# Copying two projections in time order, and multiplying them from strided reads on GpSimd

## The chip, the cores and the metric

The kernel runs on one core of one Trainium2 chip. The metric is the device time of one execution in microseconds (us), the median of several runs. Engines are named as the profile names them: PE (TensorE matmul), PEld (TensorE weight load), DVE (VectorE), ACT (ScalarE), POOL (GpSimd), SP (SyncE, which here only issues DMAs).

## What is computed

Two layers, one behind the other, on `x` and `f_logit` of shape (4, 6272, 256):

```
sig = 1/(1+exp(-f_logit));  f = lb + (1-lb)*sig;  i = 1-f
h[t] = f[t]*h[t-1] + i[t]*x[t]                       # recurrence over t, per batch and column
x1, x2, x3 = split(h @ w_proj)                       # 256 -> 3 x 256
conv = irfft(rfft(x2, S) * rfft(filter, S), S)       # circular convolution over t, S = 6272
out  = (x1 * conv * x3) @ w_out
```

## The kernel before, in words

The sequence length 6272 is 49 * 128. The convolution is done as a Fourier transform in two factors, so time t = 49*m + r is needed both as a run over t (for the recurrence) and as an array over (r, m), with m from 0 to 127 innermost (for the transform's output). Each of the four batches b passes through these stages:

- `hgrn(b)`: 13 chunks of 512 time steps. A chunk is loaded (`FL`, `XT`, two buffers each), ACT takes the sigmoid in place (L283), POOL multiplies x by it (L285, 128x1024 f32), PE transposes both (L294), ACT makes f (`fTs`, L306), DVE scans (L311) and writes h into `HA`. Then a copy called a wrap (L262 when it is POOL's, L257 when it is DVE's) puts h a second time into the buffer between the two halves of `HA`.
- `phase_p(b)`: 98 pairs of matmuls (L590) project h to x2 with weights read from `HA` by a stride of 49; ACT or DVE evict to `X2`. It waits for all scans and wraps of the batch.
- `phase_f1(b)`: first factor of the transform (L605), evicted by ACT or DVE into `A`, in `HA`.
- `mini(b)`: a small product for frequency zero (L620, L626, L630), which ends in `zm`.
- `units(b)`: 16 units u. In each, four matmuls (L649, the second factor), two DVE products with the filter `Hu` (L659, into `PP`, two buffers), one POOL copy of `zm` into `PP` (L652), 16 small matmuls back (L669) and one eviction to `Th` (L252 on ACT or L257 on DVE). After unit u comes `gate(b, u)`.
- `gate(b, u)`: for each chunk c of `GATES[u]` (10 values of m, that is 490 time steps; the last chunk has 8 and 392) and for each of two column halves `jb`: PE projects h to x1 and to x3 (L340, two matmuls each of 490 columns), ACT copies both from PSUM to `x1s` and `x3s` (L350, two buffers each), POOL writes `z = x1s * x3s` (L355) in f16 in the (r, m) layout. There are 13 chunks, so 52 ACT copies and 26 POOL products per batch.
- `phase_o(b)`: 13 groups: matmuls (L695), the DVE product with `z` (L702, which needs all of the batch's z), the projection by `w_out` (L712), eviction by ACT (L254), store.

The instruction order is written by `Plan`, a list scheduler that runs when the program is built: each `op` is given a cost in microseconds per engine allowed, and tags that it reads (`r`) and writes (`w`); the plan gives the next instruction to the engine where it can start first, by those costs. Each engine then runs its own instructions strictly in that order. A cost in the source is therefore no time of the chip, but it decides the order, and also the engine where two are allowed. PSUM is eight banks, handed out by the plan. In `hgrn(b+1)` the transposes of chunk c wait for the tag `("U", AFTER[c])`, the end of unit 2, 5, 7, 10, 12 or 15 of batch b, so that batch b+1 begins inside `units(b)`. The tag `qX` keeps the projections of `gate` in order, the tag `qT` the transposes of `hgrn`. The projections of `gate(b, u)` read the tag `("F", u)`, so they wait for the L649 matmuls of unit u.

Of the kernel before, what the change touches and what calls it, by code (L numbers as in the profile page):

```python
# [13 lines left out]
AOP = mybir.AluOpType  # L14
AF = mybir.ActivationFunctionType
# [9 lines left out]
Q = 49  # L25
# [3 lines left out]
NCHK = 13  # L29

AFTER = (2, 5, 7, 10, 12, 15)

GATES = [[u] if u < NCHK else [] for u in range(16)]
XR = 10
NEP = 128
UE = 8
# [2 lines left out]
ZS = 64.0  # L39
# [16 lines left out]
class Plan:  # L56
# [20 lines left out]
    def op(self, cost, fn, r=(), w=(), kb=0.0, table=None, take=0, src=None):  # L77
        preds = set()
        for t in r:
            if t in self.writer:  # L80
                preds.add(self.writer[t])
        for t in w:
            if t in self.writer:
                preds.add(self.writer[t])
            preds.update(self.readers.get(t, ()))
        me = len(self.ops)
        if src is not None:
            preds.add(src)
            self.ops[src]["users"].append(me)
        self.ops.append(dict(cost=cost, fn=fn, preds=preds, kb=kb, table=table, end=None,  # L90
                             eng=None, succ=[], take=take, src=src, users=[], at=None))
        for p in preds:
            self.ops[p]["succ"].append(me)
        for t in r:
            self.readers.setdefault(t, set()).add(me)
        for t in w:
            self.writer[t] = me
            self.readers[t] = set()
        return me
# [89 lines left out]
def kernel(  # L189
# [15 lines left out]
    op = plan.op  # L205
# [12 lines left out]
    W13 = konst.tile([128, 2, 512], F16, name="W13")  # L218
# [13 lines left out]
    x1s = konst.tile([128, 2, CH], F32, name="x1s")  # L232
# [5 lines left out]
    PS = psp.tile([128, 8, 512], F32, name="PS")  # L238

    def E(a, z):  # L240

        return [("E", u) for u in range(a // 1024, (z - 1) // 1024 + 1)]
# [6 lines left out]
    def copy(e, dst, src, scale=None):  # L249
        if e == "ACT":  # L250
            if scale is None:
                nc.scalar.copy(dst, src)  # L252
            else:
                nc.scalar.activation(dst, src, AF.Copy, scale=scale)  # L254
        elif e == "DVE":
            if scale is None:
                nc.vector.tensor_copy(dst, src)  # L257
            else:
                nc.vector.tensor_scalar(dst, in0=src, scalar1=scale, scalar2=None,
                                        op0=AOP.mult)  # L260
        else:
            nc.gpsimd.tensor_copy(dst, src)  # L262

    def either(n, runs=1.0):

        return {"ACT": 0.06 + runs * n / 1200.0, "DVE": 0.08 + runs * n / 960.0}

    count = dict(x=0, f=0, s=0, o=0)

# [1 line left out]
    def hgrn(b):  # L271
        for c in range(NCHK):
            t0 = c * CH
            nb = min(CH, S - t0) // 128
            n = nb * 128
            k = count["x"] % NX
            count["x"] += 1
            xt, ft = XT[:, k, 0:nb], FL[:, k, 0:nb]
            for dst, src, t in ((ft, f_logit, ("ft", k)), (xt, x, ("xt", k))):
                op({"SP": 0.5}, lambda e, dst=dst, src=src, t0=t0, n=n: nc.sync.dma_start(  # L280
                    dst, src[b, t0:t0 + n, :].rearrange("(j p) d -> p j d", p=128)),
                   w=[t], kb=n)
            op({"ACT": 0.1 + 0.213 * nb}, lambda e, ft=ft: nc.scalar.activation(  # L283
                ft, ft, AF.Sigmoid, scale=-1.0), r=["sin"], w=[("ft", k)], table="sigmoid")
            op({"POOL": 0.1 + 0.535 * nb}, lambda e, xt=xt, ft=ft: nc.gpsimd.tensor_tensor(  # L285
                xt, xt, ft, op=AOP.mult), r=[("ft", k)], w=[("xt", k)])

            late = [("U", AFTER[min(c, len(AFTER) - 1)])] if b else []
            for kh in range(2):
                cols = slice(kh * 128, kh * 128 + 128)  # L290

                def turn(e, p, src, cols=cols, nb=nb):
                    for j in range(nb):
                        nc.tensor.transpose(PS[:, p, j * 128:(j + 1) * 128], src[:, j, cols],  # L294
                                            iden[:])
                sT = op({"PE": 0.108 * nb}, lambda e, p, f=turn, s=ft: f(e, p, s),
                        r=[("ft", k), "iden"] + late, w=["qT"], take=1)
                uT = op({"PE": 0.108 * nb}, lambda e, p, f=turn, s=xt: f(e, p, s),
                        r=[("xt", k), "iden"], w=["qT"], take=1)
                j = count["f"] % 2  # L300
                count["f"] += 1
                fT = fTs[:, j, 0:n]
                t1 = HB[kh] + t0
                h = HA[:, t1:t1 + n]
                op({"ACT": 0.13 + n / 1200.0}, lambda e, p, fT=fT, n=n, kh=kh:
                   nc.scalar.activation(fT, PS[:, p, 0:n], AF.Identity,  # L306
                                        scale=nomc[:, kh:kh + 1], bias=1.0),
                   r=["om"], w=[("fT", j)], src=sT)
                init = 0.0 if c == 0 else HA[:, t1 - 1:t1]
                op({"DVE": 0.07 + 2.25 * n / 1000.0}, lambda e, p, h=h, fT=fT, n=n, init=init:  # L310
                   nc.vector.tensor_tensor_scan(h, fT, PS[:, p, 0:n], init, op0=AOP.mult,  # L311
                                                op1=AOP.add),
                   r=[("fT", j)] + ([("hn", kh, c - 1)] if c else []), w=[("hn", kh, c)],
                   src=uT)

                a, o = (t0, t0) if kh == 0 else (max(t0, S - E1), EW - S + max(t0, S - E1))
                z = min(t0 + n, E0) if kh == 0 else t0 + n
                if z <= a:
                    continue
                op({"DVE": 0.08 + (z - a) / 3840.0, "POOL": 0.1 + (z - a) / 1000.0},  # L320
                   lambda e, a=a, o=o, z=z, kh=kh: copy(
                       e, HA[:, S + o:S + o + z - a], HA[:, HB[kh] + a:HB[kh] + z]),
                   r=[("hn", kh, c)], w=E(o, o + z - a))


    def gate(b, u):
        z = zt[b % 2]
        for c in GATES[u]:
            m0 = c * XR
            nm = min(XR, 128 - m0)  # L330
            hn = [("hn", kh, i) for kh in range(2) for i in range(max(c - 1, 0), c + 1)]
            t0, n = m0 * Q, nm * Q
            for jb in range(2):
                x13 = []
                for i in range(2):
                    js = slice(i * 256 + jb * 128, i * 256 + jb * 128 + 128)

                    def mm(e, p, js=js, t0=t0, n=n):
                        for kh in range(2):
                            nc.tensor.matmul(PS[:, p, 0:n], W13[:, kh, js],  # L340
                                             HA[:, HB[kh] + t0:HB[kh] + t0 + n],
                                             start=(kh == 0), stop=(kh == 1))
                    x13.append(op({"PE": 2 * n / 2400.0}, mm,
                                  r=hn + ["W13", ("F", u)], w=["qX"], take=1))
                j = count["s"] % 2
                count["s"] += 1
                xs = [t[:, j, 0:n] for t in (x1s, x3s)]
                for i in range(2):
                    op({"ACT": 0.16 + n / 1200.0}, lambda e, p, xs=xs[i], n=n, nm=nm, i=i:
                       nc.scalar.activation(  # L350
                           xs.rearrange("p (r m) -> p m r", m=nm),
                           PS[:, p, 0:n].rearrange("p (m r) -> p m r", r=Q), AF.Copy,
                           scale=1.0 if i else ZS), w=[("x1s", j, i)], src=x13[i])
                op({"POOL": 0.12 + 2.2 * n / 1000}, lambda e, xs=xs, nm=nm,
                   zz=z[:, jb, :, m0:m0 + nm]: nc.gpsimd.tensor_tensor(  # L355
                       zz, xs[0].rearrange("p (r m) -> p r m", m=nm),
                       xs[1].rearrange("p (r m) -> p r m", m=nm), op=AOP.mult),
                   r=[("x1s", j, 0), ("x1s", j, 1)], w=[("z", b % 2, jb, c)])


# [276 lines left out]
    def units(b):  # L637
        for u in range(NU):
# [26 lines left out]
            def inv(e, ib, k=k):  # L665
# [10 lines left out]
                PS[:, ib:ib + 2, 0:392].rearrange("p a (g c) -> p c a g", g=4)),  # L676
               r=[("x2", g) for g in range(13)], w=["Th", ("Th", u)], src=i2)
            gate(b, u)


# [112 lines left out]
```

## Time and profile before

| | |
|---|---|
| median of 3 runs | 627.38 us (624.77 to 632.55) |
| the profiled execution | 630.62 us, of which the span of instructions is 628.7 us |
| mean granted TensorE clock | 0.939 |
| PE busy | 514.8 us, 82% of the span |
| ACT busy | 489.0 us, 78% |
| DVE busy | 484.3 us, 77% |
| POOL busy | 300.9 us, 48% |
| bytes moved | 117.57 MB, mean 187 GB/s |

All durations below come from that one profiled execution. Busy times of one engine count overlapping instructions fully in a row's sum, so the distance between two starts in the timeline is the truer price of an instruction in a dense row. The stages of the four batches can be read in the timeline: units from about 125 to 194, 261 to 327, 401 to 468 and 535 to 596 us; phases P and F1 ahead of them from about 100, 239, 378 and 513 us; between units and the next phase P lies `phase_o(b)` together with the rest of `hgrn(b+1)`, and the last `phase_o` ends the program.

### The profile page before, as it was taken

The page shows a single profiled execution, that of the slowest core. Times are in us where ns is not written, and L with a number is a line of the kernel's source. Part 1 is how long each engine was busy: PE and PEld are TensorE (multiplying, and loading weights), DVE is VectorE, ACT ScalarE, POOL GpSimd, SP SyncE. Part 2 cuts the span into 40 slices and gives each one's busy share as a digit, 9 for nine tenths or more (in the row PEclk, how much of TensorE's full clock was granted, in tenths as well). Part 3 has the DMA queues.
Part 4 walks back from the last instruction along what each step waited for, and adds up shares of the span by engine and source line. Part 5 has one row for each costly group of instructions (what it writes and reads, how often), then busy time and mean ns, then how long its engine had stood idle before and what let it go on. Part 6 is the DMA issues. An engine that isn't in the chain of part 4 may idle for free.

```text
span 628.7 us, 12525 instructions
## 1 busy us (share of the span) xinstructions
PE 514.8 (82%) x4821; PEld 373.3 (59%) x4821; DVE 484.3 (77%) x490; ACT 489.0 (78%) x578; POOL 300.9 (48%) x312
## 2 busy tenths in 40 slices
PE   0789977888988877888979968889889978888694
PEld 0677756734557767544557757545457768344383
DVE  8977876867888887857968997958789878757562
ACT  4777764879997667989986666989996669799834
POOL 4353452346776444155765443256884530366500
PEclk9877997979999899989999998989999989799988
DMA  9965888123768885033748984036578940234046
GB/s 317 329 231 185 282 283 263 34 84 101 234 193 233 323 302 176 27 104 105 235 145 277 313 304 138 27 103 193 159 241 304 330 157 1 78 103 129 27 168 243
DMA packets 73037, 117.57 MB, mean 187 GB/s; under 512 B 4366, under 2 KB 55634, under 8 KB 72978
## 3 DMA queue, kind: packets, MB, share of 16 engines
q1 hardware_dynamic: 72978, 116.77, 56.4%
q8 instruction: 38, 0.62, 0.4%
q14 instruction: 21, 0.17, 0.1%
HBM read 84.54 MB, written 32.11 MB: 186 GB/s over the span
## 4 chain that ended last, share of the span: by engine, by line
PE 38%; ACT 24%; DMA 13%; DVE 11%; issue 9%; POOL 4%; SPq 0%; ACTq 0%; DVEq 0%; POOLq 0%
ACT x3s L350 8%; PE PS L340 7%; ACT x1s L350 7%; PE PS L294 7%; PE PS L590 6%; DMA H<-HA 4%; ACT X L252 4%; PE PS L712 4%; PE PS L669 4%; DMA FL<-in_f_logit_dram 4%; PE PS L649 3%; DVE HA L311 3%; POOL XT L285 3%; DVE HA L257 3%; DMA XT<-in_x_dram 2%
## 5 line engine op out<-in xcount | busy, mean ns | idle before, releaser
L355 POOL TENSOR_TENSOR z<-x1s,x3s 128x490 f16<-128x490 f32 (+1 forms) x104 | 126.7, 1220 | 142.0 <-ACT x3s L350 136.1
L659 DVE TENSOR_TENSOR PP<-PS,Hu 98x1008 f16<-98x1008 f32 x128 | 147.3, 1201 | 52.9 <-ACT x3s L350 24.0
L285 POOL TENSOR_TENSOR XT<-XT,FL 128x1024 f32<-128x1024 f32 (+1 forms) x52 | 119.2, 2293 | 83.7 <-DMA XT<-in_x_dram 43.0
L311 DVE TENSOR_TENSOR_SCAN HA<-fTs,HA,PS 128x512 f16<-128x512 f32 (+1 forms) x96 | 114.7, 1205 | 26.0 <-PE PS L294 12.8
L350 ACT ACTIVATE x1s<-PS 128x490 f32<-128x490 f32 (+1 forms) x104 | 113.0, 1086 | 4.6 <-PE PS L340 4.3
L340 PE MATMUL PS<-HA,W 128*128 128x490 f16 (+1 forms) x416 | 108.9, 373 | 8.8 <-ACT x1s L350 5.3
L350 ACT ACTIVATE x3s<-PS 128x490 f32<-128x490 f32 (+1 forms) x104 | 113.9, 1095 | 0.1
L252 ACT CAST X<-PS 128x784 f16<-128x784 f32 (+2 forms) x80 | 84.5, 1070 | 22.8 <-PE PS L669 12.1
L306 ACT ACTIVATE fTs<-PS,nomc 128x512 f32<-128x512 f32 (+1 forms) x104 | 68.8, 672 | 39.3 <-PE PS L294 32.7
L294 PE MATMUL PS<-iden,FL 128*128 128x128 f32 x392 | 66.5, 293 | 19.3 <-ACT FL L283 17.1
L294 PE MATMUL PS<-iden,XT 128*128 128x128 f32 x392 | 68.3, 298 | 16.1 <-POOL XT L285 15.0
L702 DVE TENSOR_TENSOR ys<-PS,z 128x1024 fp32r<-128x1024 f32 (+1 forms) x52 | 59.4, 1151 | 18.5 <-PE PS L695 16.5
L669 PEld LDWEIGHTS <-PP 98*128 98x128 f16 x1024 | 54.6, 103 | 28.1 <-POOL PP L652 13.0
L340 PEld LDWEIGHTS <-W 128*128 128x128 f16 x416 | 36.4, 98 | 58.3 <-issue 40.3
L712 PE MATMUL PS<-Wo,ys 128*128 128x256 f32 x392 | 62.5, 304 | 6.5 <-DVE ys L702 5.3
L283 ACT ACTIVATE FL<-FL 128x1024 f32<-128x1024 f32 (+1 forms) x52 | 53.0, 1022 | 17.6 <-DMA FL<-in_f_logit_dram 17.5
L669 PE MATMUL PS<-VA,PP 98*128 98x98 f16 x512 | 57.1, 216 | 11.1 <-POOL PP L652 7.8
L294 PEld LDWEIGHTS PS<-iden,FL 128*128 128x128 f32 x392 | 49.1, 150 | 28.6 <-issue 13.4
L294 PEld LDWEIGHTS PS<-iden,XT 128*128 128x128 f32 x392 | 46.7, 150 | 29.7 <-POOL XT L285 18.8
L649 PE MATMUL PS<-HA,FT 64*128 64x512 f16 x256 | 48.6, 402 | 15.0 <-ACT x3s L350 6.5
L257 DVE CAST X<-PS 128x1024 f16<-128x1024 f32 (+2 forms) x36 | 47.0, 1331 | 17.9 <-PE PS L590 14.3
L712 PEld LDWEIGHTS PS<-Wo,ys 128*128 128x128 f32 x392 | 52.3, 199 | 12.1 <-DVE ys L702 6.8
(90 smaller groups left out, 674.5 us busy)
## 6 DMA issues: line engine op xcount, KB each, us to landing
Hu<-H SPq DMA_DIRECT2D x64, 392.0 KB
FL<-in_f_logit_dram SPq DMA_DIRECT2D x48, 512.0 KB
XT<-in_x_dram SPq DMA_DIRECT2D x48, 512.0 KB
out_dram<-X SPq DMA_DIRECT2D x24, 512.0 KB
out_dram<-osb SPq DMA_DIRECT2D x24, 512.0 KB
HA<-in_moe_filter_fft_dram SPq DMA_DIRECT2D x12, 512.0 KB
H<-HA SPq DMA_DIRECT2D x16, 196.0 KB
H<-HA SPq DMA_DIRECT2D x32, 98.0 KB
```

Source lines behind the costliest of these rows:

```text
L252: nc.scalar.copy(dst, src)
L285: op({"POOL": 0.1 + 0.535 * nb}, lambda e, xt=xt, ft=ft: nc.gpsimd.tensor_tensor(xt, xt, ft, op=AOP.mult), r=[("ft", k)], w=[("xt", k)])
L294: nc.tensor.transpose(PS[:, p, j * 128:(j + 1) * 128], src[:, j, cols], iden[:])
L306: nc.scalar.activation(fT, PS[:, p, 0:n], AF.Identity, scale=nomc[:, kh:kh + 1], bias=1.0),
L311: nc.vector.tensor_tensor_scan(h, fT, PS[:, p, 0:n], init, op0=AOP.mult, op1=AOP.add),
L340: nc.tensor.matmul(PS[:, p, 0:n], W13[:, kh, js], HA[:, HB[kh] + t0:HB[kh] + t0 + n], start=(kh == 0), stop=(kh == 1))
L350: nc.scalar.activation(xs.rearrange("p (r m) -> p m r", m=nm), PS[:, p, 0:n].rearrange("p (m r) -> p m r", r=Q), AF.Copy, scale=1.0 if i e ...
L355: zz=z[:, jb, :, m0:m0 + nm]: nc.gpsimd.tensor_tensor(zz, xs[0].rearrange("p (r m) -> p r m", m=nm), xs[1].rearrange("p (r m) -> p r m", m ...
L649: nc.tensor.matmul(PS[:, xb + e2, :], FT[rows, r, :], A[rows, es, r, :], start=(r == 0), stop=(r == 1))
L659: nc.vector.tensor_tensor(PP[:TB, k, o, :, :, 1:64], px.unsqueeze(1).broadcast_to([TB, 2, UE, 63]), hh[:, :, :, 1:64], op=AOP.mult)
L669: nc.tensor.matmul(PS[:, ib + o, pr * TB:(pr + 1) * TB], PP[:TB, k, o, n, 2 * pr:2 * pr + 2, :], v[:TB], start=(n == 0), stop=(n == 1))
L712: nc.tensor.matmul(po[:, i, :], y[:, kh, i * 128:(i + 1) * 128], Wo[:, kh, :], start=(kh == 0), stop=(kh == 1))
```

## The change

ACT no longer permutes while it copies: `x1s` and `x3s` stay in order of time, (m r), and both sides of the ACT instruction are contiguous. POOL now reads both operands with m innermost, that is by steps of 49 f32 elements (196 bytes), and writes z in runs of ten f16 values, as before. The first three chunks of a batch's gate are listed under unit 0, chunks 3 to 12 under units 1 to 10; the projections under unit 0 no longer wait for that unit's matmuls but for the last transpose of the batch (`qT`). Wraps may run on POOL alone. Four cost figures of the plan change: evictions on either engine, `fTs`, the copies of x1 and x3; the cost of the POOL product stays.

```
-GATES = [[u] if u < NCHK else [] for u in range(16)]
+GATES = [[0, 1, 2], [3], [4], [5], [6], [7], [8], [9], [10], [11], [12]] + [[]] * 5
...
-        return {"ACT": 0.06 + runs * n / 1200.0, "DVE": 0.08 + runs * n / 960.0}
+        return {"ACT": 0.15 + runs * n / 1200.0, "DVE": 0.15 + runs * n / 960.0}
...
-                op({"ACT": 0.13 + n / 1200.0}, lambda e, p, fT=fT, n=n, kh=kh:
+                op({"ACT": 0.24 + n / 1200.0}, lambda e, p, fT=fT, n=n, kh=kh:
...
-                op({"DVE": 0.08 + (z - a) / 3840.0, "POOL": 0.1 + (z - a) / 1000.0},
+                op({"POOL": 0.1 + (z - a) / 1000.0},
...
-                                  r=hn + ["W13", ("F", u)], w=["qX"], take=1))
+                                  r=hn + ["W13", ("F", u) if u else "qT"], w=["qX"], take=1))
...
-                    op({"ACT": 0.16 + n / 1200.0}, lambda e, p, xs=xs[i], n=n, nm=nm, i=i:
+                    op({"ACT": 0.15 + n / 1200.0}, lambda e, p, xs=xs[i], n=n, i=i:
                        nc.scalar.activation(
-                           xs.rearrange("p (r m) -> p m r", m=nm),
-                           PS[:, p, 0:n].rearrange("p (m r) -> p m r", r=Q), AF.Copy,
-                           scale=1.0 if i else ZS), w=[("x1s", j, i)], src=x13[i])
-                op({"POOL": 0.12 + 2.2 * n / 1000}, lambda e, xs=xs, nm=nm,
+                           xs, PS[:, p, 0:n], AF.Copy, scale=1.0 if i else ZS),
+                       w=[("x1s", j, i)], src=x13[i])
+                op({"POOL": 0.12 + 2.2 * n / 1000}, lambda e, xs=xs,
                    zz=z[:, jb, :, m0:m0 + nm]: nc.gpsimd.tensor_tensor(
-                       zz, xs[0].rearrange("p (r m) -> p r m", m=nm),
-                       xs[1].rearrange("p (r m) -> p r m", m=nm), op=AOP.mult),
+                       zz, xs[0].rearrange("p (m r) -> p r m", r=Q),
+                       xs[1].rearrange("p (m r) -> p r m", r=Q), op=AOP.mult),
```

## The prediction

> **What bounds the kernel now.** I read the page's shares and groups first, then a table by stage, then the timeline of the stage that the change touches.
>
> ```profile
> span 628.7 us, 12525 instructions
> PE 38%; ACT 24%; DMA 13%; DVE 11%; issue 9%; POOL 4%; SPq 0%; ACTq 0%; DVEq 0%; POOLq 0%
> L355 POOL TENSOR_TENSOR z<-x1s,x3s 128x490 f16<-128x490 f32 (+1 forms) x104 | 126.7, 1220 | 142.0 <-ACT x3s L350 136.1
> L350 ACT ACTIVATE x1s<-PS 128x490 f32<-128x490 f32 (+1 forms) x104 | 113.0, 1086 | 4.6 <-PE PS L340 4.3
> L350 ACT ACTIVATE x3s<-PS 128x490 f32<-128x490 f32 (+1 forms) x104 | 113.9, 1095 | 0.1
> ```
>
> No engine bounds the whole span. The chain that ended last is PE for 38% and ACT for 24%, and the ACT group that the change touches has almost no idle time ahead of it (4.6 and 0.1 us), while POOL's product waits 136.1 us for ACT. So where gates run, ACT is late. The table by stage (columns: PE, PEld, DVE, ACT, POOL busy, then granted clock, DMA share, GB/s) shows where that is:
>
> ```profile
> 125.00:194.00 69.00, 60.81 (x540) 34.84 (x538) 52.43 (x50) 64.13 (x80) 46.74 (x52) 0.95 0.53 158
> 194.00:239.00 45.00, 35.10 (x374) 30.22 (x374) 38.85 (x38) 27.43 (x36) 21.68 (x18) 0.96 0.87 292
> 261.00:327.00 66.00, 54.94 (x466) 29.71 (x465) 51.64 (x49) 59.72 (x73) 40.46 (x45) 0.97 0.47 140
> 401.00:468.00 67.00, 58.05 (x517) 33.36 (x515) 51.93 (x49) 63.21 (x79) 44.92 (x50) 0.97 0.52 158
> 513.00:535.00 22.00, 19.88 (x232) 18.37 (x233) 17.02 (x15) 18.49 (x16) 0.00 (x0) 1.00 0.03 9
> 535.00:548.00 13.00, 10.46 (x66) 4.71 (x65) 9.63 (x11) 8.81 (x10) 6.18 (x8) 0.77 0.22 63
> 548.00:596.00 48.00, 39.48 (x379) 20.62 (x378) 30.09 (x27) 47.29 (x57) 29.88 (x34) 0.99 0.31 93
> ```
>
> From 548 to 596 us, the last units stage after its start, ACT is busy 47.29 of 48 us: the stage is ACT-bound. The other units stages (69, 66, 67 us) are nearly so. The `phase_o` plus `hgrn` stage (194 to 239) keeps DMA busy 0.87, ACT only 27 of 45 us. Phases P and F1 (513 to 535) have PE and ACT both near 85 to 90% and POOL idle.
>
> **The ACT copies.** The timeline of ACT in one stretch (start, us, line):
>
> ```profile
> 562.47 0.87 ACT L252 CAST X<-PS 128x784 f16<-128x784 f32 x1
> 563.22 1.06 ACT L350 ACTIVATE x1s<-PS 128x490 f32<-128x490 f32 x1
> 564.06 1.10 ACT L350 ACTIVATE x3s<-PS 128x490 f32<-128x490 f32 x1
> 564.94 1.10 ACT L350 ACTIVATE x1s<-PS 128x490 f32<-128x490 f32 x1
> 565.81 0.88 ACT L252 CAST X<-PS 128x784 f16<-128x784 f32 x1
> 566.57 1.06 ACT L350 ACTIVATE x3s<-PS 128x490 f32<-128x490 f32 x1
> ```
>
> From start to start a copy takes 0.87 us (564.94 to 565.81) and an eviction 0.76. A unit with a gate costs ACT 4 x 0.87 + 0.76 = 4.24 us. The eleven chunks left at 548 us, with some twelve evictions, are 44 x 0.87 + 12 x 0.76 = 47.4 us, which is the stage. Only the copies are slow for their size: 490 elements take longer than 784. What a contiguous one costs stands in the evictions of `phase_o`, in the table by shape:
>
> ```profile
> L254 ACT ACTIVATE osb<-PS 128x1024 f32<-128x1024 f32 x24 | 24.5, 1021 | 14.1 <-DMA out_dram<-osb 7.6 <-PE PS L712 6.3
> L254 ACT ACTIVATE osb<-PS 128x256 f32<-128x256 f32 x2 | 0.8, 375 | 0.0
> ```
>
> (1021 - 375) / 768 = 0.841 ns per element, with 160 ns fixed; 490 elements come to 0.57 us, and with the 0.1 us that neighbours overlap (0.87 long, 0.75 apart) to about 0.5 us from start to start. That saves 0.37 us on each of 52 copies of a batch. A gated unit then costs ACT 4 x 0.5 + 0.76 = 2.8 us.
>
> **What is late next: PE, unless POOL is.** PE and DVE for one unit:
>
> ```profile
> 160.60 1.65 PE PS L340 x8
> 168.51 0.61 PE L649 MATMUL PS<-HA,FT 64*128 64x512 f16 x4
> 167.10 0.91 PEld L669 LDWEIGHTS <-PP 98*128 98x128 f16 x16
> 565.70 2.32 DVE L659 TENSOR_TENSOR PP<-PS,Hu 98x1008 f16<-98x1008 f32 x2 [0.15 <-issue]
> ```
>
> PE: 1.65 for the gate's eight matmuls, 0.61 + 0.91 = 1.52 for the unit itself, 3.17 with a gate. DVE: 2.32. So the covers end at 3.17 us where ACT now sets 4.24.
>
> **The POOL product** is the unknown. Rows for it, by shape, and the one f32 read by a long stride that the trace has (L542 reads one in 64, 256 bytes apart; min/median/max):
>
> ```profile
> L355 POOL TENSOR_TENSOR z<-x1s,x3s 128x490 f16<-128x490 f32 x96 | 118.5, 1236 | 134.0 <-ACT x3s L350 128.1 <-PE PS L340 5.5
> L285 POOL TENSOR_TENSOR XT<-XT,FL 128x1024 f32<-128x1024 f32 x48 | 116.3, 2424 | 81.5 <-DMA XT<-in_x_dram 42.2 <-ACT FL L283 24.0 <-ACT osb L254 7.9
> L285 POOL TENSOR_TENSOR XT<-XT,FL 128x256 f32<-128x256 f32 x4 | 2.9, 726 | 2.2 <-ACT FL L283 1.4 <-DMA XT<-in_x_dram 0.8
> L542 POOL CAST mX<-afs x16: 194/208/343, 47.6 to 89.4; 128x16 fp32r<-128x16 f32 x16
> L500 POOL CAST f<-iden x1: 223/223/223, 5.6 to 5.6; 128x16 fp32r<-128x16 f32 x1
> L652 POOL COPY PP<-zm 98x32 f16<-98x32 f16 x64 | 20.1, 332 | 8.7 <-PE PS L669 8.6
> ```
>
> Two contiguous f32 operands cost (2424 - 726) / 768 = 2.21 ns per element with 160 ns fixed, so 490 take 1.24 us. The present product, 1236 ns, is just that: its writes in runs of ten f16 cost nothing, and these stay. New are two reads by 196 bytes. The low end is no price: 16 strided elements of L542 take 208 ns, no more than 16 contiguous ones of L500 (223 ns, a single sample), which leaves 1.24 us. The high end is the stride that ACT pays for now: its writes are 40 bytes apart, and 0.37 us on 490 elements is 0.75 ns each. If each POOL operand paid as much, the product would take 1.24 + 2 x 490 x 0.75 ns = 1.98 us. I take 1.24 us, since L542 is the same engine reading the same type by a long stride, while ACT's price is for a write on another engine. But sixteen elements are few, and a fixed part that differs by 20 ns would hide a price, so the high end stays a rival with much weight.
>
> The Trainium skill, GPSIMD Engine Reference, section "Performance pitfalls for Q7 kernels", speaks against this change: a read whose step is over 8 bytes costs about one cycle more per element. No row here shows that; by it (an estimate, 1.2 GHz from the same page, both operands) the product would take 2.06 us and the time would be that of the first rival.
>
> With 1.24 us a gated unit costs POOL 2 x 1.24 + 0.33 = 2.8 us, under PE's 3.17. It passes PE at 1.42 us per product and today's 4.24 at 1.95.
>
> **The sum**, against the profiled execution. From 548 us in the last stage remain 10 gates (three are done earlier, not two) and 14 units: PE 10 x 1.65 + 14 x 1.52 = 37.8, DVE 14 x 2.32 = 32.5, ACT 40 x 0.5 + 14 x 0.76 = 30.6, POOL 20 x 1.24 + 14 x 0.33 = 29.4 us. PE is longest; with 2 us to fill and drain 40 instead of 48, **-8 us**. The other three units stages carry transposes too:
>
> ```profile
> 125.00:194.00 69.00, 12.87 (x84) 9.33 (x84) 0.95 0.53 158
> 261.00:327.00 66.00, 8.15 (x52) 5.81 (x52) 0.97 0.47 140
> 401.00:468.00 67.00, 11.77 (x76) 8.48 (x76) 0.97 0.52 158
> ```
>
> (L294 alone, PE busy first.) PE there: 16 x 1.52 + 10 x 1.65 + 11 = 52 us, DVE 52 as now. The start of a stage, where PE waits for `mini`, adds some 8 us that no copy shortens: 60 against a mean of 67, **-7 us** each, -21.
>
> The three early chunks go where the plan finds room after the last transpose: the tail of `hgrn`, P and F1. They bring 24 matmuls (3 x 1.65 = 5 us of PE), 12 copies (6 us of ACT) and six products, to a stretch with PE 19.88 and ACT 18.49 of 22 us busy. About half fits; I charge **+2.5 us** to each of four batches, +10. The ends are 0 (all fits) and +5 (PE's whole price).
>
> Wraps:
>
> ```profile
> L257 DVE COPY HA<-HA x50: 195/294/2474, 38.9 to 513.2; 128x512 f16<-128x512 f16 x46, 128x128 f16<-128x128 f16 x4
> L262 POOL COPY HA<-HA x50: 502/613/732, 38.9 to 512.2; 128x512 f16<-128x512 f16 x42, 128x384 f16<-128x384 f16 x4, 128x464 f16<-128x464 f16 x4
> 505.36 2.47 DVE L257 COPY HA<-HA 128x512 f16<-128x512 f16 x1
> 505.34 2.34 POOL L285 TENSOR_TENSOR XT<-XT,FL 128x1024 f32<-128x1024 f32 x1 [2.12 <-PE PS L294]
> ```
>
> A DVE wrap is 0.29 us alone and up to 2.47 beside a POOL product, and a scan may stand behind it. 50 of them become 0.61 us each on POOL, 31 us in all, in its queue between the multiplications by the sigmoid, where a wrap that waits for its scan holds up the next L285 and the transposes behind it. In the `hgrn` stage POOL is busy 22 of 45 us, so it has the room. What DVE gains on the path, some 1 us per batch, POOL's order can give back: 0, with 3 us either way. Changed plan costs move engines and order of evictions; ACT's and DVE's were both set too low by similar amounts, so 0, with 5 us either way.
>
> Sum: -8 - 21 + 10 = -19 us on 630.62, that is 611.6. The median shown is 3.2 us under the profiled execution, so the forecast is **608 us** (-3%). Two per cent, 12.5 us, is about what a measurement of this kernel can tell from no change.
>
> **Rivals.** (1) *POOL becomes the bound* (slower). Above 1.42 us each 0.1 us on the product adds 20 x 0.1 = 2 us to a units stage, 8 to the kernel; the 19 us are gone at 1.67 us. At 1.98 us the time is 627.4 + 8 x 3.1 = 652. There are two `x1s` buffers, so ACT's copies would wait for POOL, and the evictions behind them in ACT's queue, also in phases P and F1, with PE behind those. For it: ACT's own strided writes. Against it: L542 and the 136.1 us that POOL waits today.
> (2) *The gain comes only in the last batch.* The `hgrn` stages are at 0.87 DMA share with loads that two buffers and the unit tags keep from running ahead; DVE has 52 us in the middle stages and its queue is in order. If the middle stages give 1 to 2 us and the early chunks cost their whole PE price, the sum is -8 - 5 + 10, about 624 us. Against it: ACT is over 90% busy in those stages, with no second engine as full.
> (3) *The copies don't get faster*, because reading PSUM and not the strided write is slow: about 630. L252 speaks against it, with 784 elements out of PSUM faster than 490.
>
> **How the numbers follow.** Forecast 0.50 (594 to 620 with its own ends: 0 to +20 for the early chunks, 8 for wraps and plan, as much for the middle stages); rival 1 0.26 (630 to 660); rival 2 0.21; rival 3 0.03. The range that leaves out 2 in 10 takes in the forecast, rival 2 and rival 1 up to its high end: 593 to 655. Faster by over 2% (below 614.8) is most of the forecast and a little of rival 2: 0.50; within 2% (to 639.9), the rest of those and the milder part of rival 1: 0.27; slower 0.23.
>
> **What would show it.** L350 near 0.57 us; ACT busy about 100 us less; L355 at 1.24 us (right), over 1.67 (rival 1, with `POOL z` as the releaser ahead of ACT's L350); PE with the smallest gaps in the units stages; the last one near 52 us, the middle ones near 60; P plus F1 2 to 3 us longer, with L340 in it; no L257 COPY beside scans. A product over 1.42 us makes the prediction wrong first, the early chunks on the path to phase P second.

## The result and the profile after

| | before | after |
|---|---|---|
| median | 629.96 us (4 runs) | 606.81 us (4 runs, 604.48 to 613.48) |
| ratio | | 0.9638, 95% interval 0.9553 to 0.9724 |
| profiled execution, span | 630.62, 628.7 us | 613.48, 611.7 us |

The changed kernel is 3.6% faster; the forecast was 608 us. The profiled execution of the changed kernel was a disturbed one (clock 0.917, all others 604 to 608 us), so its stage times are about 1% long. The page's engine rows and groups after:

```profile
span 611.7 us, 12552 instructions
PE 505.6 (83%) x4821; PEld 377.6 (62%) x4821; DVE 470.2 (77%) x450; ACT 409.6 (67%) x568; POOL 396.0 (65%) x362
L354 POOL TENSOR_TENSOR z<-x1s,x3s 128x490 f16<-128x490 f32 (+1 forms) x104 | 200.1, 1938 | 61.7 <-ACT x3s L350 58.8
L354 POOL TENSOR_TENSOR z<-x1s,x3s 128x490 f16<-128x490 f32 x96 | 187.4, 1965 | 60.2 <-ACT x3s L350 57.3 <-PE PS L668 2.7
L350 ACT ACTIVATE x1s<-PS 128x490 f32<-128x490 f32 (+1 forms) x104 | 60.4, 581 | 43.3 <-PE PS L340 22.1
L350 ACT ACTIVATE x3s<-PS 128x490 f32<-128x490 f32 (+1 forms) x104 | 59.6, 573 | 5.3 <-PE PS L340 5.0
```

The copies are at 0.58 us, as computed. The product is not: 1.96 us for 490 elements (the second L354 row; 1.94 in the mean over both shapes), where I took 1.24. (Line numbers behind the gate are one lower than before: L354 is the product, L668 the small matmuls of a unit, L711 the projection by `w_out`.) The last units stage, by windows (PE, PEld, DVE, ACT, POOL busy, clock, DMA share, GB/s), then POOL and ACT in its second half, and DVE in its first:

```profile
540.00:557.00 17.00, 17.00 (x189) 9.73 (x186) 15.90 (x15) 14.42 (x25) 16.15 (x15) 0.99 0.50 155
557.00:577.00 20.00, 17.34 (x204) 9.94 (x200) 14.99 (x14) 14.17 (x25) 20.00 (x17) 1.00 0.29 92
```
```profile
562.03 1.99 POOL L354 TENSOR_TENSOR z<-x1s,x3s 128x490 f16<-128x490 f32 x1
563.93 0.35 POOL L651 COPY PP<-zm 98x32 f16<-98x32 f16 x1
564.09 1.98 POOL L354 TENSOR_TENSOR z<-x1s,x3s 128x490 f16<-128x490 f32 x1
```
```profile
564.05 0.58 ACT L350 ACTIVATE x1s<-PS 128x490 f32<-128x490 f32 x1 [0.73 <-POOL z L354]
566.11 0.58 ACT L350 ACTIVATE x1s<-PS 128x490 f32<-128x490 f32 x1 [0.31 <-POOL z L354]
```
```profile
541.41 22.77 DVE L658 TENSOR_TENSOR PP<-PS,Hu 98x1008 f16<-98x1008 f32 x20 [1.03 <-issue]
```

ACT no longer bounds. Until 557 us PE (17.00 of 17) and DVE (15.90; twenty products with `Hu` in one run of 22.77 us) do, with POOL close behind at 16.15; from 557 to 577 POOL is busy 20.00 of 20 us, and ACT's next `x1s` copy waits for the product two before it. So POOL did become a bound, in the second half of the stage. POOL's products of the early chunks show why it is not later still:

```profile
505.67 4.09 POOL L354 TENSOR_TENSOR z<-x1s,x3s 128x490 f16<-128x490 f32 x2
518.92 7.67 POOL L354 TENSOR_TENSOR z<-x1s,x3s 128x490 f16<-128x490 f32 x4 [9.15 <-ACT x3s L350]
531.00 3.79 POOL L354 TENSOR_TENSOR z<-x1s,x3s 128x490 f16<-128x490 f32 x2 [4.41 <-ACT x3s L350]
```

Eight of the batch's 26 products run between 505.7 and 534.8 us, in phases P and F1, where POOL had nothing to do before, and while `mini` runs; before, three began ahead of the batch's first unit. Stage lengths tell where the time went. They are taken from each kernel's timeline, between the first L590 matmul (phase P), the first L669 (first unit), the first L712 (phase O) of each batch and the end of the span (line numbers of before; the four batches in order, in us; e1 to e12 are the runs below):

```
                      to 1st P | P to 1st unit           | units, to phase O       | O to the next P  | O to end
before                 101.6   | 31.0  29.7  31.2  29.7  | 62.9  63.9  62.3  55.2  | 43.5  45.2  41.3 | 31.2
after                  102.7   | 30.3  30.0  30.0  30.0  | 60.5  54.6  58.0  43.0  | 44.2  51.5  43.7 | 33.2
e1 POOL contiguous      98.4   | 29.8  28.9  28.5  28.6  | 54.0  49.6  52.0  39.8  | 45.7  52.7  42.9 | 30.0
e2 layout alone        105.1   | 32.3  31.5  31.7  29.9  | 66.9  67.4  66.6  50.3  | 41.7  44.7  43.6 | 30.5
e6 plan knows 1.97 us  100.4   | 30.7  30.1  31.4  30.0  | 57.0  51.5  58.1  44.3  | 40.9  46.5  40.7 | 31.0
e8 five chunks early    99.8   | 31.9  32.4  32.5  31.7  | 49.1  50.7  50.7  39.2  | 56.0  50.2  53.7 | 30.4
e4 gates undone         96.9   | 33.3  31.5  31.6  31.0  | 62.1  58.4  63.3  51.6  | 42.9  50.3  42.9 | 31.2
e5 wraps undone         98.0   | 30.6  29.9  30.1  30.0  | 59.3  55.5  61.3  43.1  | 46.0  49.0  42.9 | 32.7
e10 write by stride     99.2   | 30.4  30.2  30.7  30.7  | 60.8  56.5  62.9  47.5  | 43.3  52.3  44.0 | 32.6
e12 costs undone       101.7   | 29.8  29.9  29.8  30.0  | 59.2  53.0  62.1  42.8  | 42.7  52.1  43.7 | 32.2
```

Each row is one profiled execution. Ahead of the first phase P the changed kernel, e1 and e10 run the same instructions in 98.4 to 102.7 us, so a difference of a few us between two rows can be chance.

From before to after the units stages give 2.4 + 9.3 + 4.3 + 12.2 = 28 us. The early chunks cost phases P and F1 nothing (-1.3 us in all). 9.4 us are given back between phase O and the next phase P.

### The profile page after: what moved, and what is told of

It reads as the page before. It is cut to its first block, busy times and chain, and to the rows that moved or that the text cites. A ratio compares the mean times of both kernels' runs of the same rounds, so it can differ in the third digit from the quotient of the medians.

```text
span 611.7 us, 12552 instructions
## 1 busy us (share of the span) xinstructions
PE 505.6 (83%) x4821; PEld 377.6 (62%) x4821; DVE 470.2 (77%) x450; ACT 409.6 (67%) x568; POOL 396.0 (65%) x362
## 5 line engine op out<-in xcount | busy, mean ns | idle before, releaser
L354 POOL TENSOR_TENSOR z<-x1s,x3s 128x490 f16<-128x490 f32 (+1 forms) x104 | 200.1, 1938 | 61.7 <-ACT x3s L350 58.8
L311 DVE TENSOR_TENSOR_SCAN HA<-fTs,HA,PS 128x512 f16<-128x512 f32 (+1 forms) x96 | 114.7, 1206 | 47.6 <-PE PS L294 38.2
L285 POOL TENSOR_TENSOR XT<-XT,FL 128x1024 f32<-128x1024 f32 (+1 forms) x52 | 118.0, 2271 | 42.7 <-DMA XT<-in_x_dram 22.5
L340 PE MATMUL PS<-HA,W 128*128 128x490 f16 (+1 forms) x416 | 111.3, 388 | 4.1 <-ACT x1s L350 3.3
L252 ACT CAST X<-PS 128x784 f16<-128x784 f32 (+2 forms) x82 | 82.4, 1013 | 32.4 <-PE PS L668 27.3
L294 PE MATMUL PS<-iden,XT 128*128 128x128 f32 x392 | 70.8, 306 | 35.5 <-POOL XT L285 31.5
L262 POOL COPY HA<-HA 128x512 f16<-128x512 f16 (+3 forms) x100 | 59.0, 598 | 61.6 <-DVE HA L311 59.1
L350 ACT ACTIVATE x1s<-PS 128x490 f32<-128x490 f32 (+1 forms) x104 | 60.4, 581 | 43.3 <-PE PS L340 22.1
L294 PE MATMUL PS<-iden,FL 128*128 128x128 f32 x392 | 67.6, 297 | 20.9 <-ACT FL L283 18.6
L294 PEld LDWEIGHTS PS<-iden,XT 128*128 128x128 f32 x392 | 49.2, 155 | 51.1 <-POOL XT L285 36.5
L668 PEld LDWEIGHTS <-PP 98*128 98x128 f16 x1024 | 57.0, 105 | 31.7 <-POOL PP L651 19.1
L701 DVE TENSOR_TENSOR ys<-PS,z 128x1024 fp32r<-128x1024 f32 (+1 forms) x52 | 59.3, 1154 | 19.1 <-PE PS L694 13.8
L668 PE MATMUL PS<-VA,PP 98*128 98x98 f16 x512 | 58.3, 219 | 16.8 <-POOL PP L651 16.0
L711 PE MATMUL PS<-Wo,ys 128*128 128x256 f32 x392 | 63.5, 308 | 5.9 <-DVE ys L701 3.8
L294 PEld LDWEIGHTS PS<-iden,FL 128*128 128x128 f32 x392 | 50.3, 153 | 27.8 <-issue 15.5
L350 ACT ACTIVATE x3s<-PS 128x490 f32<-128x490 f32 (+1 forms) x104 | 59.6, 573 | 5.3 <-PE PS L340 5.0
L711 PEld LDWEIGHTS PS<-Wo,ys 128*128 128x128 f32 x392 | 53.7, 204 | 9.8 <-issue 3.4
```

The source lines that it names most:

```text
L340: nc.tensor.matmul(PS[:, p, 0:n], W13[:, kh, js], HA[:, HB[kh] + t0:HB[kh] + t0 + n], start=(kh == 0), stop=(kh == 1))
L350: nc.scalar.activation(xs, PS[:, p, 0:n], AF.Copy, scale=1.0 if i else ZS),
L354: zz=z[:, jb, :, m0:m0 + nm]: nc.gpsimd.tensor_tensor(zz, xs[0].rearrange("p (m r) -> p r m", r=Q), xs[1].rearrange("p (m r) -> p r m", r= ...
L668: nc.tensor.matmul(PS[:, ib + o, pr * TB:(pr + 1) * TB], PP[:TB, k, o, n, 2 * pr:2 * pr + 2, :], v[:TB], start=(n == 0), stop=(n == 1))
L701: nc.vector.tensor_tensor(y, PS[:, cb:cb + 2, 0:rn * 128], zr[:, :, r0 * 128:(r0 + rn) * 128], op=AOP.mult),
L711: nc.tensor.matmul(po[:, i, :], y[:, kh, i * 128:(i + 1) * 128], Wo[:, kh, :], start=(kh == 0), stop=(kh == 1))
```

## The experiments

All ratios are against the kernel before on the same chip. The differences in us below are between medians; some runs were on other chips, and by the ratios the same differences come out up to 3 us otherwise.

| run | median us | ratio, 95% |
|---|---|---|
| changed kernel | 606.81 | 0.964, 0.955 to 0.972 |
| e1 POOL contiguous | 582.25 | 0.928, 0.914 to 0.942 |
| e2 layout alone | 646.01 | 1.029, 1.014 to 1.044 |
| e3 layout undone | 622.34 | 0.993, 0.989 to 0.997 |
| e4 gates undone | 626.39 | 0.998, 0.993 to 1.004 |
| e5 wraps undone | 606.18 | 0.961, 0.953 to 0.969 |
| e6 true cost | 597.64 | 0.950, 0.944 to 0.955 |
| e7 one operand | 595.21 | 0.944, 0.937 to 0.951 |
| e8 five early | 613.27 | 0.976, 0.969 to 0.983 |
| e10 write by stride | 621.97 | 0.988, 0.983 to 0.993 |
| e11 one operand, true costs | 602.57 | 0.957, 0.949 to 0.966 |
| e12 costs undone | 611.65 | 0.971, 0.964 to 0.978 |

**e1: the product without its price**, same instruction order. The kernel leaves out the permutation of z to (r, m).

```
-                       zz, xs[0].rearrange("p (m r) -> p r m", r=Q),
-                       xs[1].rearrange("p (m r) -> p r m", r=Q), op=AOP.mult),
+                       zz, xs[0].rearrange("p (r m) -> p r m", m=nm),
+                       xs[1].rearrange("p (r m) -> p r m", m=nm), op=AOP.mult),
```

> The changed kernel in the same instruction order, but POOL reads both operands contiguously: the permutation to (r, m) is left out, z holds its values in another order. L354 goes from 1.96 to 1.24 us. Theory A (the strided product is late only where products pile up at the end of a units stage, the rest hides behind DVE and PE): 590 to 602 us, some 1 to 4 us less per stage, most in the last one, and DVE with PE as the next bound. Rival B (my prediction's slope, 8 us of the kernel per 0.1 us of product above 1.42): the product costs 43 us now, so about 563 us. Rival C (POOL is hidden altogether): 605 us, no change.

582.25 us, below theory A and far above rival B. The group by shape, and the last units stage:

```profile
L354 POOL TENSOR_TENSOR z<-x1s,x3s 128x490 f16<-128x490 f32 x96 | 117.6, 1232 | 96.4 <-ACT x3s L350 95.6 <-PE PS L668 0.6
```
```profile
511.00:547.00 36.00, 35.92 (x374) 20.23 (x375) 33.54 (x30) 29.33 (x49) 23.40 (x32) 0.95 0.46 139
```

With the product at 1.23 us PE is busy 35.92 of 36 us and DVE 33.54: what the prediction said would bound the kernel at that price does. The price of the stride is 606.8 - 582.3 = 24.5 us for 0.73 us per product, 3.3 us of the kernel per 0.1 us: not hidden, and not 8 us either. Rival C falls too.

**e2: the layout alone**, on the kernel before, with its order (the ACT and POOL lines of the diff and nothing else).

> The kernel before in its own order (GATES, wraps and costs as before), with the layout of the change alone: ACT copies contiguous, POOL reads by 196 bytes. L350 0.58 us, the product 1.96. Theory A (layout gives most of the gain, order the rest): 610 to 620 us, with POOL ahead of ACT's copies in the waits of the units stages. Rival D (with one gate per unit a gated unit costs POOL 2 x 1.96 + 0.33 = 4.25 us, what ACT cost before, so the layout alone gives nothing and the gain comes from the order): 625 to 632 us.

646.01 us, slower than before: theory A falls, rival D was still too mild. The timeline of POOL and the waits over the span:

```profile
579.40 3.85 POOL L354 TENSOR_TENSOR z<-x1s,x3s 128x490 f16<-128x490 f32 x2
583.18 0.34 POOL L651 COPY PP<-zm 98x32 f16<-98x32 f16 x1
583.35 3.89 POOL L354 TENSOR_TENSOR z<-x1s,x3s 128x490 f16<-128x490 f32 x2
587.16 0.34 POOL L651 COPY PP<-zm 98x32 f16<-98x32 f16 x1
```
```profile
ACT x1s L350 <- POOL z L354: 43.2, 61, 2.0
```

A unit takes 587.16 - 583.18 = 3.98 us on POOL without a gap; ACT waits 43.2 us for it. The first three units stages, where POOL also has L285 and wraps, last some 67 us in place of 63; the last one gets shorter, 50.3 in place of 55.2. This is the mechanism of the prediction's rival 1, met in the order of before. Not all of the loss is the product's, though. The profiled span is 13.5 us longer than before, and only 7 us of that lie in the units stages. Another 6 lie ahead of the first phase P and in the phases P and F1 up to their last matmul, where both kernels run the same instructions and no product.

**e3: the layout undone**, in the changed kernel's order.

> The changed kernel in the same instruction order, with the layout of before: ACT writes by 40 bytes (0.87 us from start to start), POOL reads contiguously (1.24 us). Theory A: ACT bounds the units stages again, but four chunks of each batch lie in phases P and F1, so 615 to 625 us. Rival D (the gain is the order's): 605 to 610 us.

622.34 us, as theory A. ACT's copies are back at their old length (by shape):

```profile
L350 ACT ACTIVATE x3s<-PS 128x490 f32<-128x490 f32 x96 | 105.7, 1101 | 1.1 <-PE PS L340 0.9
L350 ACT ACTIVATE x1s<-PS 128x490 f32<-128x490 f32 x96 | 104.6, 1090 | 12.6 <-PE PS L340 11.4 <-POOL z L355 1.2
```

With e2 this makes a square: order alone 0.993, layout alone 1.029, both 0.964. Neither part is worth much without the other; by the medians the layout gains 15 us in the new order and loses 16 in the old, the latter in part by chance, as e2's stages show.

**e4: the early chunks undone** in the changed kernel (old `GATES`, `("F", u)` for every u).

> The changed kernel with the GATES of before and each projection behind its unit's matmuls: no early chunks. Theory A: 26 instead of 18 products of 1.96 us must pass POOL in the units stage, and the last stage from its first unit to phase O gets 43 + 8 x 1.96 = 59 us at most, some 8 to 15 us more; in all 615 to 625 us. My prediction's term (early chunks cost 2.5 us per batch in P and F1 and save 5 us of PE in units): 607 to 615 us.

626.39 us: 19.6 us more. The last units stage has POOL at 45.25 of 50 us, and ACT waits for it (over the span; the changed kernel first, then e4):

```profile
544.00:594.00 50.00, 43.22 (x432) 23.34 (x432) 33.68 (x30) 33.66 (x59) 45.25 (x39) 0.94 0.33 98
```
```profile
ACT x1s L350 <- POOL z L354: 18.6, 24, 3.4
```
```profile
ACT x1s L350 <- POOL z L354: 53.7, 68, 3.5
```

So of this change's parts the early chunks are what makes the layout pay, for without them the ratio is 0.998: they move POOL work to where POOL is idle.

**e5 and e12: wraps and costs undone**, each alone (the `+` lines of the diff turned back).

> The changed kernel with wraps on DVE or POOL as the plan likes, at the costs of before. My prediction's term for the wraps was 0, with 3 us either way: 604 to 610 us. Theory A2 (POOL's queue is the bound, and DVE wraps beside a POOL product take up to 2.5 us and hold up the scans): DVE copies appear again with a median near 0.3 and a maximum over 2 us; POOL loses some 25 us of work but DVE gains more, 605 to 615 us.

> The changed kernel with the plan's costs of evictions, fTs and the x1, x3 copies as before (0.06, 0.08, 0.13, 0.16 us fixed instead of 0.15, 0.15, 0.24, 0.15). My prediction's term was 0, with 5 us either way: 602 to 612 us. Theory J (with true costs the plan overlaps better; between layout alone, 646.0, and gates undone, 626.4, only wraps and these costs differ, so some of those 20 us are theirs): 612 to 620 us.

606.18 us: the wraps are worth nothing that the intervals can tell, although some of DVE's copies are as slow as before or slower (min/median/max):

```profile
L257 DVE COPY HA<-HA x44: 195/294/4370, 36.7 to 501.9; 128x512 f16<-128x512 f16 x39, 128x128 f16<-128x128 f16 x4, 128x464 f16<-128x464 f16 x1
```

611.65 us for the costs: some 5 us, at the edge of my term (0, 5 either way) and of what the intervals separate. Between e2 and e4 wraps and costs together made 20 us; which of the two, in that order, was not run.

**e6: the plan is told the product's length.** `"POOL": 0.12 + 2.2 * n / 1000` becomes `0.15 + 3.72 * n / 1000`.

> The changed kernel with the plan's cost of the POOL product set from 0.12 + 2.2 n/1000 (1.20 us) to 0.15 + 3.72 n/1000 (1.97 us, what the trace shows). Theory A2 (POOL's queue is the bound in units, and what counts is how much of its work lies in phases P and F1; the plan's picture of it is secondary): 600 to 612 us. Rival E (the plan, knowing the length, orders the wraps, the multiplications L285 and the products so that the transposes wait less for L285): 592 to 600 us.

597.64 us, rival E. Its profiled span is 19.1 us shorter than the changed kernel's (the medians differ by 9.2), and the stage table puts 11.3 us of that between phase O and the next phase P. PE's waits in the transposes for POOL's multiplication L285, over the span, in the kernel before, in the changed kernel, in e1 and then here:

```profile
PE PS L294 <- POOL XT L285: 15.0, 13, 2.5
```
```profile
PE PS L294 <- POOL XT L285: 31.5, 19, 4.0
```
```profile
PE PS L294 <- POOL XT L285: 30.5, 20, 4.0
```
```profile
PE PS L294 <- POOL XT L285: 20.8, 17, 3.1
```

The length of the product is not what makes L285 late. With products of 1.23 us (e1) PE waits as long for it, and the three stretches from O to P last 141.3 us, against 139.4 in the changed kernel and 139.6 with products of 2.50 us (e10). In the order of before they last 130 us, with the strided product too (e2). So the 9.4 us belong to the order that the plan wrote. POOL's queue in the second of these stretches of the changed kernel shows how: ahead of L285 stand wraps, and these wait for their scans (L311):

```profile
333.82 0.61 POOL L262 COPY HA<-HA 128x512 f16<-128x512 f16 x1 [1.69 <-DVE HA L311]
334.39 2.35 POOL L285 TENSOR_TENSOR XT<-XT,FL 128x1024 f32<-128x1024 f32 x1
338.91 0.61 POOL L262 COPY HA<-HA 128x512 f16<-128x512 f16 x1 [2.16 <-DVE HA L311]
339.48 2.37 POOL L285 TENSOR_TENSOR XT<-XT,FL 128x1024 f32<-128x1024 f32 x1
```

In that stretch (322.3 to 373.8 us) POOL's wraps wait 18.0 us for scans, and no product begins before its last 0.2 us; in the same stretch of the kernel before they wait 7.8 us, in e6 8.1. PE's waits for L285 are 11.4 us there and were 4.5 before: 6.9 us more, in a stretch that is 6.3 us longer. e6 shows that another order has the time back. Which part of the new order costs it stays open: with the gates, the wraps or the costs alone undone (e4, e5, e12) the three stretches still last 136.1, 137.9 and 138.5 us.

**e8: five chunks early** (`GATES = [[0, 1, 2, 3, 4], [5], ...]`).

> The changed kernel with five chunks under unit 0 instead of three, ungated by that unit's matmuls. Theory A2: POOL is idle for a part of phases P and F1 still, about 7 of 25 us before the fourth phase P's end; more of its work there leaves less in units: 600 to 606 us. Rival G (POOL has as much work there as ACT's evictions and the two x1s buffers allow, and PE's phase P is then held up): 606 to 612 us.

613.27 us, beyond rival G. The units stages get 26 us shorter than after, P and F1 8 us longer, and 20 us go to the stretch between O and P. More of the next batch's `hgrn` is left for it (27 multiplications L285 begin in the three stretches, 22 in the changed kernel), and transposes wait still longer for L285 (over the span, against 31.5):

```profile
PE PS L294 <- POOL XT L285: 40.1, 24, 4.2
```

**e7 and e11: one operand strided**, x3 permuted by ACT and x1 in order of time; e11 tells the plan the measured prices of this form.

```
-                           xs, PS[:, p, 0:n], AF.Copy, scale=1.0 if i else ZS),
+                           xs.rearrange("p (r m) -> p m r", m=nm) if i else xs,
+                           PS[:, p, 0:n].rearrange("p (m r) -> p m r", r=Q) if i else PS[:, p, 0:n],
...
-                       xs[1].rearrange("p (m r) -> p r m", r=Q), op=AOP.mult),
+                       xs[1].rearrange("p (r m) -> p r m", m=nm), op=AOP.mult),
```

> The changed kernel, but x3 is permuted by ACT as before (write by 40 bytes) and x1 stays in order of time, so POOL reads one operand by 196 bytes and one contiguously. If each strided operand has its own price (0.73 us for two, 1.96 against 1.24), L354 takes 1.60 us; if the slower operand sets it, 1.9 us. ACT gets 52 x 0.37 us = 19 us back per... in all 38 us of work. Theory A2 (POOL is the bound, 3.4 us of the kernel per 0.1 us of product as between 606.8 and 582.3): 594 to 600 us at 1.60, if ACT (still under 80% busy) stays hidden. Rival F (ACT and POOL together cost what they cost apart): 606 or more.

> As the run with one operand strided (x3 permuted by ACT, product 1.48 us, 595.2 us), with the plan told the measured prices: product 0.15 + 2.72 n/1000, x3 copy 0.865 us. If what the true cost brought with two operands (606.8 to 597.6) comes again: 584 to 590 us. If it was only worth something where POOL is late: 592 to 597 us.

595.21 us: the lowest of the versions that compute the whole, 1.9% under the changed kernel (e6 lies within its interval). The product and the strided copy:

```profile
L355 POOL TENSOR_TENSOR z<-x1s,x3s 128x490 f16<-128x490 f32 x96 | 141.6, 1480 | 93.8 <-ACT x3s L350 86.5 <-PE PS L649 7.1
L350 ACT ACTIVATE x3s<-PS 128x490 f32<-128x490 f32 x96 | 102.1, 1063 | 5.1 <-PE PS L340 4.7
```

One strided operand costs 0.25 us, the second 0.49; I had expected equal prices (1.60 us). Handing half of the permutation back to ACT uses ACT's room: ACT is busy 445.0 us here, 76% of the span, against 409.6 and 67% in the changed kernel. True costs here gave 602.57, against the expectation of either theory: a truer cost is no sure gain in a list scheduler. Its interval overlaps that of e7; why it was worse was not settled.

**e10: POOL reads contiguously and writes by 256 bytes** (`zz.rearrange("p r m -> p m r")`, both operands `"p (m r) -> p m r"`).

> The changed kernel with the permutation moved to POOL's write: it reads x1s and x3s contiguously in order of time and writes z, f16, by steps of 256 bytes. Same instruction order. Theory H (POOL has one write per two reads, so a slower write hides behind them): L354 1.24 to 1.4 us and 582 to 590 us, as with the permutation left out. Rival I (a strided write costs as much as a strided read or more; L652 writes 32 such values in 0.33 us, which over a fixed 0.19 is 4 ns each): L354 1.6 to 3 us, 595 to 640 us.

```profile
L354 POOL TENSOR_TENSOR z<-x1s,x3s 128x490 f16<-128x490 f32 x96 | 223.5, 2504 | 50.8 <-ACT x3s L350 47.8 <-PE PS L668 2.7
```

Rival I: 2.50 us a product, 621.97 us. From e1 over e7 and the changed kernel to e10 the product takes 1.23, 1.48, 1.96, 2.50 us and the kernel 582, 595, 607, 622 us: 2.4 to 2.8 us per 0.1 us in the last two steps. The first step is steeper, 5.2, but e7 also gives ACT its strided copy back.

**e9: the stride by itself.** Products and copies added at the end of the changed kernel.

> The changed kernel with POOL instructions added at its end, each twice: products of 480 f32 elements at steps of 1, 2, 3, 4, 8 and 48 elements for both operands, at 48 for one, at step 1 with a write by 96 bytes, copies of 480 at steps of 1, 2, 4 and 48, and copies of 16 at steps of 1 and 64. Theory K (a price per element as soon as the step is over 8 bytes, as the Trainium skill has it, and the same beyond): steps 1 and 2 take 1.22 us, steps 3 to 48 about 1.93; copies 0.6 and about 0.95. Theory L (the price grows with the step): step 3 and 4 lie between 1.22 and 1.93. For 16 elements theory K gives 12 ns more at step 64 than at step 1, so that a row of that size could not have told the price.

The second pass, when less else ran: products with both operands at steps of 1, 2, 3, 4, 8, 48 elements (L773 to L778), one at 48 (L779), contiguous reads with a write by 96 bytes (L780); copies at steps 1, 2, 4, 48 (L783 to L786); sixteen elements at steps 1 and 64 (L787, L788):

```profile
590.96 1.21 POOL L773 TENSOR_TENSOR z<-XT,FL 128x480 f16<-128x480 f32 x1
592.25 1.43 POOL L774 TENSOR_TENSOR z<-XT,FL 128x480 f16<-128x480 f32 x1
593.76 1.70 POOL L775 TENSOR_TENSOR z<-XT,FL 128x480 f16<-128x480 f32 x1
595.53 2.00 POOL L776 TENSOR_TENSOR z<-XT,FL 128x480 f16<-128x480 f32 x1
597.61 1.89 POOL L777 TENSOR_TENSOR z<-XT,FL 128x480 f16<-128x480 f32 x1
599.58 1.80 POOL L778 TENSOR_TENSOR z<-XT,FL 128x480 f16<-128x480 f32 x1
601.46 1.43 POOL L779 TENSOR_TENSOR z<-XT,FL 128x480 f16<-128x480 f32 x1
602.97 2.33 POOL L780 TENSOR_TENSOR z<-XT,FL 128x480 f16<-128x480 f32 x1
605.36 0.58 POOL L783 CAST z<-XT 128x480 f16<-128x480 f32 x1
606.01 0.61 POOL L784 CAST z<-XT 128x480 f16<-128x480 f32 x1
606.68 1.02 POOL L785 CAST z<-XT 128x480 f16<-128x480 f32 x1
607.76 0.98 POOL L786 CAST z<-XT 128x480 f16<-128x480 f32 x1
608.81 0.20 POOL L787 CAST z<-XT 128x16 f16<-128x16 f32 x1
609.07 0.21 POOL L788 CAST z<-XT 128x16 f16<-128x16 f32 x1
```

Copies follow theory K: next to free at 8 bytes, 0.4 us more at 16 and the same at 192, 0.8 to 0.9 ns per element. Products follow theory L up to 16 bytes (1.21, 1.43, 1.70, 2.00) and cost no more beyond. The 16-element rows differ by 10 ns for a stride of 256 bytes. These are single rows, each run twice in one execution, and with the step the runs between two jumps get shorter too (480 elements at step 1, ten at step 48); the two were not varied apart.

## Why the prediction came out, step by step

The number was right by luck: wrong terms cancelled. e1 is the kernel that I summed up, with the product at 1.24 us: it takes 582 us, not 608. The sum fell 26 us short, and the price of the stride, which I had set to nothing, is 24.5 us. Where it fell short, the stages of e1 tell: the units stages give 49 us for the 29 of the sum, P and F1 are 5.8 us shorter where it had 10 more, and the stretches from O to P are 11 us longer, for which it had no term. By the prediction's own signs rival 1 came true, a product over 1.67 us with `POOL z` as the releaser ahead of ACT's L350 (18.6 us); only its time of 652 us did not.

- **The copies** (0.57 us, 0.5 from start to start): right; 0.58, and 0.46 from start to start (ACT as a whole is busy 79 us less, not 100):

```profile
505.01 0.58 ACT L350 ACTIVATE x3s<-PS 128x490 f32<-128x490 f32 x1
505.47 0.59 ACT L350 ACTIVATE x1s<-PS 128x490 f32<-128x490 f32 x1
```

- **The product, 1.24 us**: wrong, 1.96. The step that failed is "I take 1.24 us, since L542 is the same engine reading the same type by a long stride". e9 shows that a copy of 16 elements has 10 ns to show a price of 0.85 ns per element; that row could never have told, and I had noted as much. The other row, ACT's strided write, gave 1.98, within 1%, and that is luck as well: it charges each operand 0.37 us, where e7 shows 0.25 for one and 0.49 for the second, and POOL's own strided write costs 1.27 us (e10). The Trainium skill's rule (GPSIMD Engine Reference, "Performance pitfalls for Q7 kernels"), a price of about one cycle per element for a read whose step is over 8 bytes, gave 2.06 as an estimate. For copies the trace agrees: 8 bytes cost 0.03 us and 16 bytes 0.44 on 480 elements, 0.9 ns each. For products it does not: 8 bytes already add 0.22 us to 1.21.
- **The slope of rival 1** (8 us per 0.1 us above 1.42): wrong in the new order, 3.3. It took all 20 products of a units stage as the pace. In fact PE and DVE paced the first half of the last stage, and only the second half was POOL's. In the order of before (e2) the time came near, 646 for 652, but the rival had summed up the new order, and only half of e2's loss lies in the units stages.
- **The early chunks, +2.5 us per batch**: wrong in sign. They cost P and F1 nothing and undoing them costs 19.6 us. I had priced their PE and ACT work and not seen that their worth lies in POOL's work (eight products, 16 us per batch, run ahead of the first unit where three did before), though the row for 513 to 535 us showed POOL at 0.00.
- **The units stages, -8 and three times -7**: -12.2 and -2.4, -9.3, -4.3; the sum 28 for 29 hits by the same cancelling. With the product at 1.23 us (e1) they give 8.9, 14.3, 10.3 and 15.4, 49 in all. Too cautious in part was the start of the stage, counted at 8 us that could not shrink: from the first unit's small matmuls to the fifth's it is 13.3 to 14.3 us before and 10.2 to 11.5 in e1. The rest of the surplus was not traced to a term.
- **Between O and the next P, no term**: 9.4 us longer, by the new order and not by the product's length (e1, e10). The paragraph on wraps had the mechanism, a wrap that waits for its scan and holds up the next L285, and then charged 0. Rival 2 had this place right, for another reason: transfers, where it was POOL's queue.
- **Wraps, 0**: right in the total (e5). **Costs, 0 with 5 either way**: about 5 (e12), with intervals that overlap.

## What to carry to other kernels

Price an unknown access by a row with enough elements: sixteen elements cannot show a nanosecond each. Where no row has the access at its size, add it to a kernel and measure it, as e9 does; the strided row of another engine came near here by luck. When work moves to an idle engine, look for the stretch where that engine is idle and whether the order lets the work get there; here the same layout gains 15 us in one order and loses time in the other. A right total proves no term: run the kernel that has exactly the price that was assumed (e1 here). The same run tests a cause: a wait that is as long with short products does not come from long ones.

## What the runs showed of the hardware

GpSimd's price for a stride is not additive over the operands of a product: one operand of 480 f32 by 192 bytes adds 0.22 us to 1.21, two add 0.6, and steps of 16 bytes (0.8) are no cheaper than steps of 192. A strided f16 write is dearer than two strided reads (2.33 us by 96 bytes against 1.80 for the reads by 192; with 490 elements 2.50 by 256 against 1.96 by 196), although there is one write to two reads.
